# Other layouts for K and Q in DRAM, a single reciprocal load, wider gelus, new planner prices and a new order in a fused attention and mixer kernel

## The chip, the cores and the metric

The kernel runs on one core of a Trainium2 chip. The metric is device time in microseconds of one execution. The kernel before takes 1880.47 us, the median of three runs (1879.46 to 1881.93).

## The reference

The input x has 2048 tokens of 640 channels, in float32. It is normalised once (xn), and the output is x plus an attention block on xn plus a mixer block on xn.

```python
xn = layernorm(x)
# A: 32 heads of 20 channels
q, k, v = split(xn_n @ wqkv)              # xn_n = layernorm(xn)
o = softmax(q k^T * 20**-0.5) v           # per head, 2048 x 2048 scores
A = o @ wo
# B: spatial shift and MLP
h  = gelu(layernorm(xn) @ w1)             # 640 x 640
hs = shift(h, channels in 4 groups, tokens by +1, -1, +2, -2) @ w2
x1 = xn + hs
B  = x1 + gelu(layernorm(x1) @ w3) @ w4   # 640 x 1536 and 1536 x 640
out = x + A + B
```

## The kernel before

**Work and tiling.** TensorE multiplies fp32 numbers in a reduced format, so an operand is split into a high and a low part ("split": a rounding copy for the high part, a subtraction for the low part), and a product is three products (high-high, high-low, low-high). Two half-height products run side by side in the array ("twins"). Attention runs over 32 blocks: a block is a pair of heads and half of the tokens as queries (`HALF` = 1024), and has 32 units of work. A unit has two score products per head pair (`s`, followed by an exponential on ScalarE, ACT), two products that only look for the row maximum of a block that comes 14 to 43 units later (`pm`, followed by a maximum on VectorE, DVE), and one group of eight products with V (`pv`). Between these stand the products of everything else, as fill: Q, K and V (`ps_q`, `ps_k`, `psv`), w1, w2, w3, w4 (`ps`), and at the end wo (`pso`, `psl`).

**What goes through DRAM.** The Q and K projections are split, and both parts go into the DRAM tensors `qd` and `kd`, one per 128 channels, with the layout channel, block of 512 tokens, part, token. Per block, `load_q` fetches the two heads' Q for one half of the tokens into one of three tiles `zq`, three blocks ahead. Per pair of heads, `load_k` fetches all tokens of K into one of two tiles `kpack`. Both place three copies per head at different partitions: for Q the slots are high, low, high, for K high, high, low. A head has 20 rows; where they cross a boundary of 128 channels, each copy takes two transfers. The weights are split once and kept in DRAM: `prep` loads a piece (`ph_w`), rounds it on ACT or DVE, subtracts on GpSimd (POOL) and stores it as `wd_w`.

**End of a block.** `block_end` stores the block's four rows of sums (`od`), loads them again spread over 128 partitions (`sm`), takes reciprocals on DVE (`rc`), stores them (`rcd`), loads each of the four rows repeated over 32 partitions (`rb`, four transfers), multiplies on POOL and stores the result in `onm`.

**w1.** `w1_tile` computes 128 output channels for 2048 tokens, in two rounds of 1024. Each round evacuates two tiles into `pre` (two buffers of 1024 columns), multiplies by a row factor, runs one gelu on ACT, splits and stores to `hsd`. The gelu needs another table on ACT than the exponential, so each change loads a table. The last w1 tile and the last Q tile are computed in two visits, one round each.

**What sets the order.** All transfers are issued by one queue, SyncE (SP), in order. Nothing is ordered by hand except one string: a planner collects all operations, with a price each and the operations on which they depend, and simulates the engines in time. When an engine is free it takes the ready operation with the lowest key. For TensorE the string `ORDER` says at each step which kind comes next (`s` scores, `p` products with V, `m` maxima alone, `d` anything else). The planned order is then emitted on each engine. A transfer has a price for its issue on SP, a time on a shared bus (`xfer`) and a lateness (`late`: 3000 ns for the weight pieces and the end of a block, 1500 ns for Q and K), after which its users count as ready. The price of an issue is 375 ns, plus 100 ns from 128 runs and 130 ns more from 256 (line 620).

Line 356 holds every TensorE group, line 324 nearly every other operation, line 344 the small memsets with which the second half of a pair of twins waits for the first.

Of the kernel before, what the change touches and what calls it, by code (L numbers as in the profile page):

```python
# [21 lines left out]
P = 128  # L22
# [89 lines left out]
    "ddsdssdddssddsddssppppsdsddsdssddsddddsdddsddsddsdsddsdsdddsspdpppsddsdsdsddsdsddsddsdsdddsspssspppsdsddsdsdsd"
    "sddsddsdsddddsssdddsddsdddsddsdsddssddppppsdsdddsdssdddsddsddsdsddssdsddspsddsddsddsddsddsddspdsddsddsppppdsds"
    "ddsdsddsdsddsdspssdddsdsddsdsddsddsdsdddssdpspppsdsdddsdddddsdspssdddsdsdssdddsddsdsdsddsspssppsspssdddssddsdp"
    "dpssddddsdddsdsdddsdsdddssdddsddddsdsdddsddddssppsdddsdsdsdsdddsddsdsddssddppppssdddsdsdsddsdsddsdsddsdddddsds"
    "dsdsdsdsppppdsddsdssdddssdddsdddsdsdsdsddsdsdsddspssspsdsdddsdsppdddsddsddsdsddssdsdsdsddsddsdsppppssddsdsdsdd"
    "dsspdpsdsdddsdspdsdsddsdsddsdsdddsspssdddsddsdsdsdsdddsdsddsddddsdsppppsddssdddddsdsdsddssdddsdsdddssdddsddsds"
    "dsdpsddddsspppdsddsdsddssdsdsdddsspsspppsdsddssddsddssdddsdsddsddsddsdddssddsdsdddssppppdsdsdddsdsdddsdsddssdd"
    "sdsddssdddssppppsdsdddssddsdsdddsddsdddsssdddsdsddddsdsdddsdsddsssppppssdddsdsdsddsddsdsdsdsdddssppppsddsdsdsd"
    "ddssddsddsdsdsddddsddsdsdsdsdsddspdpppssddsdddssdsdddsdsdsddsddsdsdsddsdsppppsdsdddssdsddddssddsddddsssdddsddd"  # L120
    "ssddsddddsdsdsdpssspppddsdddsddsddsdsdsdsdddssdsddsdsddsdsppsddsdsddsdsddspsspssspssspssspsssdpssspssspssspsss"
    "psdsdddssdddddddsddddsssddddddsdddsdddssddddddddsdsdddddsdsdddppsddsddddsdddddsddddddddddsdsdddddddsdsppsddddd"
    "dddddsdsddddsddddddssppppdsddsddddddsssddddddsddddsdddddddsddddddsddppddddddsdddsddddsddsdsdddsdddddssddddddds"
    "ppddssdddsddsdddddsddsdssddddddsdddsdsdddddssddddddddddppppssdddsddsdddsddsddsdddsdsddsdddsddsdddddsddsppsspss"
    "spsdddsddsdddsdsddddddssddddssddddssdddddssdddddsddddsdppsdsdsppsssdddddsdddsppddsssdsssppssddddsdddsdddddsddd"
    "sssddddddddssddsdddddsddsdddsddssddsdsddsdddspppppsdsdddsdsddddsdsdddsddddddsddsdddddsddddssddddsddddsdsdddsdd"
    "dspppddddsdssdddddsdddddssdddsdsddsdsdsdsddsddsddsppppssdddssddsdsdddssddsdsddsdspdpppdsdssdddsddsddsdsdsddsdd"
    "sdddsddsdsdsdsddsdspppsdsdddssdddsdsdddsdddsdsddddssppppsdddsdsdddddddsddddsspssdddsdsdsddsddssddsdsdddssppsss"
    "ppsddsdsddsdsddsdsdsddsdddssddsdsdddssppppdsdsddssdddsdsddddsdsdsddsdsdddsdsdsdddssppppssddsddsddsddssdsddsddd"
    "sdddsdsdddsddsddsdddsddpppdsdddsdspssddsdddsdsddsdsdddsddsddsdddssddsdsddsdsppssppssdddsddsddssddsdsddsdddsspp"  # L130
    "ppdsdddsdssdddsddssddsddddsssddddsdddsddsdsddsdddspssppsspssssspssspssspssspssddddddssdsdddddsdddssdddddsdsdsd"
    "dddsddsddsppppsdsdddsdddssdddsddddsdsddsdsddsdddddsdddddsddsdddddssppdppdssddddsdddssdddsdddsddsdsddsdsddddddd"
    "dsddddddddddssdddddsddsddddsddddddddddddsddppppsdddsddddsddddssddddssdddsddddsdsdddsdddsdsppppsdsdddsdsddddsdd"
    "sdsdddsdddsdsddsdddsdsdddsdddddddddsdpppddsdddddddssddddsddsddpsdsddddssdddddsddsdsdddddsdsdddddsddsdddspdsdsp"
    "sdddssdddsddsdddsdddddddddsddsdppssspssddpssspsssssppsdsdddddddsspddssssspssspsssdddddsdsddsdssdddsdsddsppsddd"
    "sddsddsddddssddddddsdddsddsdddsdddddssppppdddddsddsddddssddddddsdddddddsdddddddssdddsddsddsddddsdddddddsdddsdd"
    "dsddddddsppdddddsdsdsdsddsddsdddssppppsdsddssddsddsdsdsddddddsssdddddssddsdsddsddsddsdppsssppsdsddssddsddsdsdd"
    "sdsdsddsdspppsdsddsdsddsddsdsddsddsddsppppdsddsddsddddddsdsdddsdspssdddsdsdsddsdsddsdsdsdddssppppssddsdsdddsds"
    "ddssdddsdddsssdddsdddsdsddssddsdddssdppppsdsddssddsdsddsdsddsdsddsdsppsdsddsdsddsdsdddsdsdddddsdddsddddsdspppp"
    "ddsdsdddsdsppsdsdsdsddsddsddssdddssddsdddddsdddssdsddsddsdddssppppssdddssdddsdsdsddsddsdddssddddsdsdsdddsspppp"  # L140
    "sdsdsdddsdssddsddsddsdsdddssdsdddsdspsssppssspssspsdpssspsdddsddspsddsdsddsddsdddsdddsddddddsddsdddsddsdsdsddd"
    "sppppddsdddsddsddddddsdsddsddsddddddddsddddsdddddddddddsdddssdsdddddsddddddsddsddddsdddsdddddsdsdppppssddddsds"
    "dddddssddddssdddsddsddddsdddsddddsdsddsdddppppdsdsdddddsddddsddsdsddddsdsddddsdddsddddsdssdddsdddppppsddddssdd"
    "dddsddsdsddddsdddsdddsddsdddssdddsdsdddsddsppppsddsdsddsddddsdddsdddsddsdddsdsddsddddsddsddsddsddsdppppsdsdddd"
    "dssdddsdddsdsddddsdsdddddsdsddsddsdddsdddddssppppsddsddsddddsddsdddssddddsdddddsddsdsdddddssdddddssddppppsdsdd"
    "sdddsddsdsddddddssdddddssddddssdddddsdddsddssddppppdsdsdsddddddssddsddsdddsdddddsddsdsddddssddddsddddssppppsdd"
    "dsdsdddssdddddsdddsdsdsdddddsdddssdddddsdsdddsddsppppsdddssdddddsdsddddsdddsddsdddsddsdsddddssdddsdddsddsdpppp"
# [1458 lines left out]
```

## Time and profile before

| | |
|---|---|
| median of three runs | 1880.47 us |
| the profiled execution | 1878.9 us |
| its span, first to last instruction | 1876.7 us |
| mean granted clock of TensorE | 0.994 |
| TensorE products (PE) busy | 1841.3 us, 98% |
| weight loads (PEld) busy | 1286.3 us, 69% |
| VectorE (DVE) busy | 1517.7 us, 81% |
| ScalarE (ACT) busy | 1389.4 us, 74% |
| GpSimd (POOL) busy | 446.9 us, 24% |
| moved by DMA | 257.80 MB, on average 137 GB/s |

A row of the profile names line, engine, operation, the tile written and the tile read, and the count. "Idle before" is the time an engine stood still before an operation, with the operation or transfer that ended the wait. The chain of waits follows the last instruction back to what released each step. A window gives the busy time of the engines in a stretch of the span, with the granted clock and the mean share of the 16 DMA engines that were busy. SPq is the queue of SyncE that issues the transfers; the times of its rows are those of the issue, not of the transfer.

### The profile page before, as it was taken

The page shows a single profiled execution, that of the slowest core. Times are in us where ns is not written, and L with a number is a line of the kernel's source. Part 1 is how long each engine was busy: PE and PEld are TensorE (multiplying, and loading weights), DVE is VectorE, ACT ScalarE, POOL GpSimd, SP SyncE. Part 2 cuts the span into 40 slices and gives each one's busy share as a digit, 9 for nine tenths or more (in the row PEclk, how much of TensorE's full clock was granted, in tenths as well). Part 3 has the DMA queues.
Part 4 walks back from the last instruction along what each step waited for, and adds up shares of the span by engine and source line. Part 5 has one row for each costly group of instructions (what it writes and reads, how often), then busy time and mean ns, then how long its engine had stood idle before and what let it go on. Part 6 is the DMA issues. An engine that isn't in the chain of part 4 may idle for free.

```text
span 1876.7 us, 44340 instructions
## 1 busy us (share of the span) xinstructions
PE 1841.3 (98%) x17153; PEld 1286.3 (69%) x17153; DVE 1517.7 (81%) x2696; ACT 1389.4 (74%) x2545; POOL 446.9 (24%) x665
## 2 busy tenths in 40 slices
PE   9999999999999999899999999999999999999998
PEld 7976776666666757567666757675777777776677
DVE  8888888897888989877779996778778778778624
ACT  5278777887888886668888776888677777778762
POOL 5112114423323223211112211112221222212211
PEclk9999999999999999999999999999999999999999
DMA  5764656536464586545325563344514242243402
GB/s 195 192 187 143 159 143 185 141 113 178 123 169 138 152 256 206 169 150 179 104 73 165 147 180 106 100 119 147 132 57 104 89 110 85 70 141 119 144 13 113
DMA packets 234243, 257.80 MB, mean 137 GB/s; under 512 B 60521, under 2 KB 175673, under 8 KB 234033
## 3 DMA queue, kind: packets, MB, share of 16 engines
q1 hardware_dynamic: 234032, 254.98, 46.2%
q8 instruction: 135, 2.21, 0.5%
q14 instruction: 76, 0.61, 0.1%
HBM read 151.64 MB, written 103.25 MB: 136 GB/s over the span
## 4 chain that ended last, share of the span: by engine, by line
PE 85%; DMA 6%; DVE 5%; ACT 1%; SPq 1%; POOL 1%; issue 1%; DVEq 0%; ACTq 0%; POOLq 0%
PE ps L356 24%; PE pv L356 22%; PE s L356 13%; PE pm L356 12%; PE psv L356 3%; PE pso L356 3%; PE ps_k L356 3%; PE ps_q L356 3%; DVE mx L324 3%; DMA ph_w<-in_B_w_dram 2%; SPq L324 1%; PE psl L356 1%; DMA kpack<-kd 1%; DMA sm<-od 1%; ACT p L324 1%
## 5 line engine op out<-in xcount | busy, mean ns | idle before, releaser
L324 DVE TENSOR_REDUCE mx<-pm 128x1 f32<-128x512 f32 x2048 | 1271.4, 682 | 215.5 <-PE pm L356 128.6
L324 ACT ACTIVATE p<-s 128x512 f32<-128x512 f32 x2048 | 1106.5, 604 | 199.7 <-PE s L356 78.5
L356 PE MATMUL s<-zq,kpack 62*128 62x512 f32 x2048 | 756.4, 409 | 14.0 <-ACT p L324 4.9
L356 PE MATMUL pm<-kpack,zq 60*128 60x512 f32 x2048 | 756.6, 409 | 8.4 <-ACT p L324 4.5
L356 PE MATMUL pv<-p,v 128*32 128x512 f32 x4096 | 487.3, 599 | 0.3
L356 PEld LDWEIGHTS s<-zq,kpack 62*128 62x128 f32 x2048 | 363.2, 186 | 119.4 <-DVE mx L324 30.7
L356 PEld LDWEIGHTS pm<-kpack,zq 60*128 60x128 f32 x2048 | 364.3, 186 | 104.2 <-DVE mx L324 30.0
L356 PE MATMUL ps<-xT,w_w 64*128 64x512 f32 x2040 | 329.6, 395 | 1.2 <-ACT p L324 1.2
L356 PEld LDWEIGHTS pv<-p,v 128*32 128x32 f32 x4096 | 120.8, 110 | 231.3 <-issue 198.6
L356 PEld LDWEIGHTS ps<-xT,w_w 64*128 64x128 f32 x2040 | 210.8, 188 | 37.4 <-issue 7.1
L324 POOL TENSOR_TENSOR ob<-ob,obq 128x512 f32<-128x512 f32 x96 | 125.2, 1304 | 322.3 <-ACT obq L324 284.7
L356 PE MATMUL ps<-xT 64*128 64x320 f32 x1632 | 170.6, 308 | 0.1
L356 PEld LDWEIGHTS ps<-xT 64*128 64x128 f32 x1632 | 146.8, 186 | 13.2 <-issue 2.5
L324 ACT COPY obq<-pv 128x512 f32<-128x512 f32 x83 | 48.8, 588 | 125.2 <-PE pv L356 124.9
L344 POOL MEMSET scratch<- 1x1 f32 x134 | 12.9, 96 | 458.7 <-PE ps L356 294.2
L356 PE MATMUL ps<-xT,gT 64*128 64x320 f32 x1152 | 121.9, 307 | 0.0
L356 PEld LDWEIGHTS ps<-xT,gT 64*128 64x128 f32 x1152 | 104.1, 186 | 8.0 <-issue 1.7
L356 PE MATMUL psv<-wv,xT 64*128 64x320 f32 x960 | 93.4, 309 | 0.8 <-ACT xT L324 0.8
L356 PEld LDWEIGHTS psv<-wv,xT 64*128 64x128 f32 x960 | 82.0, 186 | 8.4 <-issue 3.0
L356 PE MATMUL ps_q<-xT,w_q 64*128 64x512 f32 x480 | 83.2, 400 | 0.0
L356 PE MATMUL ps_k<-xT,w_k 64*128 64x512 f32 x480 | 80.3, 397 | 0.9 <-POOL scratch L344 0.9
L356 PE MATMUL pso<-wos,oT 64*128 64x320 f32 x768 | 67.5, 308 | 0.0
(182 smaller groups left out, 1393.2 us busy)
## 6 DMA issues: line engine op xcount, KB each, us to landing
zq<-qd SPq DMA_DIRECT2D x156, 80.0 KB
kpack<-kd SPq DMA_DIRECT2D x78, 160.0 KB
w_w<-wd_w SPq DMA_DIRECT2D x48, 256.0 KB
gd<-pre SPq DMA_DIRECT2D x8, 1536.0 KB
g<-gd SPq DMA_DIRECT2D x64, 192.0 KB
wd_w<-ph_w SPq DMA_DIRECT2D x34, 320.0 KB
xT<-wd_w SPq DMA_DIRECT2D x34, 320.0 KB
vd<-vst SPq DMA_DIRECT2D x32, 256.0 KB
```

Source lines behind the costliest of these rows:

```text
L324: o.insts = [getattr(e, m)(val(out), *[val(x) for x in ins], **{k: val(v) for k, v in kw.items()})]
L344: o.insts = [nc.gpsimd.memset(scratch.get(), 0.0)]
L356: o.insts = [nc.tensor.matmul(out.get(), lhsT.get(), rhs.get(), **kw) for out, lhsT, rhs, kw in products]
```

## The change

Five things change.

1. `qd` and `kd` get the layout channel, half of the tokens, part, 1024 tokens. A load of K then reads two runs of 4 KB per row instead of four of 2 KB, a load of Q one run instead of two. A store of 512 tokens writes two runs of 2 KB per row instead of one of 4 KB. Where a head's 20 rows lie in one tensor, its first two copies of Q (high and low) come in one transfer, whose DRAM side runs over part, row, token.
2. The four loads of `rb` become one, whose DRAM side runs over 4 rows, 32 repeats, 512 columns.
3. In `w1_tile` one buffer `pre` of 2048 columns stands for a whole column tile, and the gelu runs once per visit: over 2048 columns for the first four tiles, over 1024 twice for the last one.
4. The planner has other prices: own issue times for several transfers, other limits for the rest, and other prices for a few DVE operations (`bn_stats`, `bn_aggr`, one `tensor_scalar`).
5. `ORDER` is another string of the same length, 7039 letters, with the same number of each letter.

```diff
 ORDER = (
-    "ddddddddddddddddddddddddddddddddddddddddddddddddddddddddddddddddddddddddddddddddddddddddddddddmddddddddddddddd"
...
+    "ddddddddddddddddddddddddddddddddddddddddddddddddddddddddddddddddddddddddddddddddddddddddddddddddddddddddmdmddd"
...
-    def dma(o, i, nbytes, es=2560, **kw):
+    def dma(o, i, nbytes, es=2560, iss=None, **kw):
         n = nbytes / es
-        op_ = pl("dma", 375.0 + 100.0 * (n >= 128) + 130.0 * (n >= 256), "dma_start", o, i,
+        op_ = pl("dma", iss or (375.0 if n < 128 else 425.0 if n < 256 else 630.0), "dma_start", o, i,
                  xfer=1.1 * (8.0 + 0.0375 * es) * math.ceil(n / 16), **kw)
...
-    qd = [dt([P, 4, 2, 512], F32R, f"qd{c}") for c in range(ND)]
-    kd = [dt([P, 4, 2, 512], F32R, f"kd{c}") for c in range(ND)]
+    qd = [dt([P, 2, 2, HALF], F32R, f"qd{c}") for c in range(ND)]
+    kd = [dt([P, 2, 2, HALF], F32R, f"kd{c}") for c in range(ND)]
...
-            pl("dve", 402.0, "bn_stats", st[:, j, :], src[:, j * 320:(j + 1) * 320])
-        pl("dve", 81.0, "bn_aggr", mv, st)
+            pl("dve", 357.0, "bn_stats", st[:, j, :], src[:, j * 320:(j + 1) * 320])
+        pl("dve", 110.0, "bn_aggr", mv, st)
...
-        o = dma(raw[:, :n].rearrange("p (k c) -> p k c", k=k), src, n * 512, 4 * n // k)
+        o = dma(raw[:, :n].rearrange("p (k c) -> p k c", k=k), src, n * 512, 4 * n // k, 480.0)
...
-                kept[nm, tb] = dma(_f(dst[:, tb]), _f(hl), 524288, 4096)
+                kept[nm, tb] = dma(_f(dst[:, tb // 2, :, tb % 2 * 512:tb % 2 * 512 + 512]), _f(hl), 524288, 2048, 560.0)
...
+        pres = {}
+
         def w1_tile(nm, w, ts=(0, 2)):
             c = int(nm[3:])
+            if c not in pres:
+                pres[c] = wp.tile([P, S], F32, tag="pre", name=f"pre1_{c}", bufs=1)
+            pre = pres[c]
             for t2 in ts:
-                pre = wp.tile([P, 512 * W1B], F32, tag="pre", name=f"pre1_{c}_{t2}", bufs=W1N)
...
-                pl("act", c_act(512 * W1B, False), "activation", pre, pre, AF.Gelu_apprx_tanh, table="gelu")
-                for b in range(W1B):
-                    tt = t2 + b
+                if t2 != ts[-1]:
+                    continue
+                a = pre[:, ts[0] * 512:(t2 + W1B) * 512]
+                pl("act", c_act((t2 + W1B - ts[0]) * 512, False), "activation", a, a, AF.Gelu_apprx_tanh, table="gelu")
+                for tt in range(ts[0], t2 + W1B):
...
 def load_k(pair):
-                        rdma(_f(t[b:b + n, s]).rearrange("p (c t) -> p c t", c=4), _f(src[r0:r0 + n, :, part, :]), n * S * 4)
+                        rdma(_f(t[b:b + n, s]).rearrange("p (c t) -> p c t", c=2), _f(src[r0:r0 + n, :, part, :]), n * S * 4, 4096)
 def load_q(blk):
-                for slot, part in enumerate(SLOT_Q):
+                slots = list(enumerate(SLOT_Q))
+                if n == DH:
+                    b = 64 * e
+                    rdma(_f(t[b:b + 2 * DH, :]), _f(src[r0:r0 + n, qh]).rearrange("p q t -> q p t"), n * HALF * 8, 4096)
+                    slots = slots[2:]
+                for slot, part in slots:
                     b = 64 * e + slot * DH + o
-                    rdma(_f(t[b:b + n, :]).rearrange("p (c t) -> p c t", c=2),
-                         _f(src[r0:r0 + n, qh * 2:qh * 2 + 2, part, :]), n * HALF * 4)
+                    rdma(_f(t[b:b + n, :]), _f(src[r0:r0 + n, qh, part, :]), n * HALF * 4, 4096)
...
-        for r in range(4):
-            adma(rb[32 * r:32 * (r + 1), :], rcd[blk, r:r + 1].to_broadcast([32, 512]), 65536, LATE)
+        adma(rb, rcd[blk].unsqueeze(1).to_broadcast([4, 32, 512]), 262144, LATE)
         pl("pool", c_pool(512), "tensor_mul", rb, ob, rb, port=True)
```

More of the change, by code (lines that the diff above doesn't have):

```diff
@@ new lines @@
+    "dmddddmddmdddddmddddmddddddmdddddddddddmddddddddddmddddddddmmmddddddddddddddddddmddmddddddddddmmdddddddddddmdd"
+    "dddddddddmddddddddmmmddddddddddddddddddddmddddddddmddmmddddddddddddddddmdddddddddddddmddmdddddddmdddddddddddmd"
+    "ddmdddddddddmsddddsddddddddsdddddsdddsddsdddsdddsddssdddsddddssdddddsddmdddsddsdsdddmsppppsdsddssdddsdssdddsds"
+    "dsddsdsdsddsdsdddsmppppsddsddssddsddsdsddsddsddssddsdsddsddmsdpssppdssddddsdsddspsdsdddsdsdsddsddssddsdddssppp"
+    "psddsddssddsddsdsdddssdddsspsspppsdsddssddsddsdsddsdsddddsssddddsdsddsdsdsddsdsppssdddspsssppssspsdsdddddsdspd"
@@ new lines @@
+    "psddsddddddsssddddsddddddsddsdddddsddddsdddsdssdddddssdddddssddddsddddsdsdppppdsdsdsdddsddddsdddddsssdddddddsd"
+    "dssdddsdddsppppsdddssdsddddsddddsdddssddddssddddsdddsdddssdpssspppsdddsdssddddddssdddddssddsdddsdddddssddddddd"
+    "dsddssddppppddssdddddddsssdddddddsddsddddddsddsddsddddsdsdsddddsdsppppdssdddsddsddddsddddsdddddsddddsddsdsdddd"
+    "ssddddsdsddsdddsddddssppppsddddssddddsdssddddssdddssddsddssdddsddssddsddddsppppssdddsddssdddssdddssdddsdsppdss"
+    "dddsddsddsdsddsddsddsdsdpppssspsdsddsdsppsdsdsdsdsddsdsdddsdssddssdddssdddssddsdsspdddsdspppssdddsdsddsdsddsds"
@@ new lines @@
+    "dsdsdddssppppssdsdddssdddssdddssddsddddsdsdddsddsdsddsdsdppppsddssddsdssddsdddsdsdsdddddsdsdsdppsssppdsddsdddd"
+    "ddddsddsdddsssddddsddssddsddsdsdsddsdsppppssddsdsddsdsddsdddsdsdsddssddsdsddsdddssppppssdddssddsdsddddsdsddsdd"
+    "ssdddsdsdsdsddpppssddddsddsdsddsdsddsdsdddddsspssdsdsdsdsddppppsddsddssddssdssdddddssddsdsdspssdppsspdssddsdsd"
+    "psdddddsdsddddsddsdddssdddsddsddsdddsdsdddsdspppssddsddsddsddssddsdsdddsdsdppppsdsddsddsdsdsdddssdsdddddsddsds"
+    "dsddsdsppppsdsddssdddsdssddddssddsdddssdsddsdsddspssspssddddsddsdddsdppdsdddssdsdsdsdsdsdsdddssppppssddsdsdsdd"
@@ new lines @@
+    "dsspdpssddddsdspdsdsdddsdpsddssdddssdsddsdsddsdddssddsdsdddssppppssdddssddsddsddsdsdsddddsssddddddsdssdddsdsdd"
+    "sdsdppppssddsddsddsddsdssddsdddsdssddsppppsdsdsddsdsddsdsdddsddsdsdssdsdsdsddsdddssdpdpppsddssddssddsdsddsdsdd"
+    "spssddpsdsppsdsdsddsdddsddddsdddddsdddsssdddddsdsddssdddssddsdsdppsssppsdsdsdsdddsdsddsdsdsdsddsdsppppsdsddsds"
+    "dsdddsdsddsddsdsdddsdddsdsdsddsdspdpppssddddsdssddsdsddsdsddsdsdddsdsdsdsppppdsdssdddsdsddsdsdsdddddsssdddddsd"
+    "ssdddsddsddsdsdpssspppddsdsddddddssddsdsdddssdddsdssddsddssppssdddsdsdddsspsspssspssspssspssspdssspssspssspsss"
@@ new lines @@
+    "pssddddsddsddddsdddddsssddddsdddddddsddsddddsddddsdddddsddsddppppsdsdddssdddsddsddddddddsddsddddsdddddddssdddd"
+    "dsddddddddddsdsdddddsppppsdddsddddddsssdddddddsdsdddddddsddddddddsddppdddsddddsddddsddddsddsdddsdsdddsddddddds"
+    "ppsddsdddddsddsddddsddssdddsdsdddsdsdddsddddddddddssddddpppsspssdddsdddsddsddddsdddssdddddsdddsdddsddddppsssps"
+    "sspsddddsddsdddsddddsddssdddsdddsdddsdddsddddsdddddsddsppsssddppssdsdddddddsspddspssssspdpsdsdsddsdsdddddsddsd"
+    "ddsssddddsdddddsdsdsddddddddsdsddsdddsdssddddpppppsdddsdsddddsdddddddsdddddsdsdddsddsddddssdddsddddsdsdddsddsd"
@@ new lines @@
+    "dspppsddddddsdsddddsddddssdddsdsddssdddsdsddsddssdppppssddsddsddssdddsdsdsdsdddssppppdsddsdssdddsdddssddsdddsd"
+    "ddsdsddsddsdsdsddsdsdddsspppssdddsddsddsddsddsddsddsppppsddddsddddsdddsdsdddspsdsddssddsddsddssddsdsddsdsppsss"
+    "ppdsdsddssdddssdddssdddsddssdsddsddsdsppppdsdsdsdsddsdsdddsdddsdsddsdsdsddsdsdsddsdsppppdssddsddsdsddsdsdsddds"
+    "ddsddsddsddsdsdsdddsdddssdppppdsdddsddsdsdsdddsdsddddsdsdsddsdsddsdsppppsdsddssdddssdsddsddsddsddssdddsddssddp"
+    "pppddsssddddsdsdsddsdddddsssddddsddssdddsdsdsddddssssppssppsssspssspssspssspsddsdsdddddsdsdddsdddssddsdddddsdd"
@@ new lines @@
+    "ssddddddssppppsdsddsdsdddddsddsddddssdsddddsddsddddsdddsdsppdsddddsddsdddsdddsdddsppsddsddsdsddddssddddddsddds"
+    "ddddddsddddddssdddddddsdsdddddddddddddddsddppppdsdsddsdddddsdsdddddssddddsddsddsdddsddddssppppsdsdsdsdddsddddd"
+    "sdsdddssddsddsdddddsdddsdddddddddssddpppddsdddddddsddsdddddsdpsdsdsdddsdddsdddsddsddsdddsddsddddsddddsdspssddp"
+    "sddsdsddsdddsddsdddddsdddddddsdsppspssspssddpssspdsdddsddddsspsspddsssssspssspssddddsdsddssdddsdsdsddsdsppsdsd"
+    "ddsddddsdsdddsdddddsdddsdsdddddssddddsppppddsdsddddddsdsdddsddddddddssdddddsdsddddssdddsdddsddddssdddddsdddddd"
@@ new lines @@
+    "dssddddddddsppppsddsdddddddsdsppsdddsdddsdsdddsddssddsddsddddsssddddsdsddddsdsddssdddspppssspssdddssddsdsdddss"
+    "ddsdsddsdspppsdsddsdsddsddsdsddsddsddspdpppsddsddsddddddsdsddddsspssdddssdddssddsdsddsdsddsdsppppssdddsdsdsdsd"
+    "dsdddsdsdddsssdddsddsddsddsdsddsdsdsdppppsdsddsdsdsddsdsddsdsdsddsdsppsdsdddsdsdddsdsddsdsdddsdddsddddssdppppd"
+    "ddsdsdddsdsppdsdsdsdsdddsdsdsdsdddsdsdddsddsddsdddsdsdsdsddsdsppppsdsddsdsddssddsdddssdddsdddsdsddsdsddsdspppp"
+    "sdsddsdsddssddddssdddssddsdsddsddsdspssspssspppssssdpssspsdsddddddsspsdsddsddddsdsdsddsddddddsdsdddsddddsdddsd"
@@ new lines @@
+    "sppppdssdddsdddsdddddsdddssddddddsdddsddddddsdddddsddddsdddddsdsddddddddddsdssdddsdddddddddppppddddsssddddddds"
+    "ddsddddsdddsddsddsddddsdddsdsddsddsddddssppppdssddsdddddssdddddsdsdddddsdsdddsdddsddddsddssddsddppppdssddsddsd"
+    "ddddsddddsddsdsddddddsddsdsddddsdsddddssddppppssddddssdddsddsddddddssddddddsdsdddssdddddssdddddssdppppsdsddddd"
+    "dssdddddsddsdsddddsddssdddddsdddssdddsddsddsppppsddsddssdddsddddddsddsddsddsddddsdsdsdddddsddsddddssppppddssds"
+    "ddddddsdsdsdddsdddsddddsdsddddsdsddddsddsdsdddsppppdsddsddsddsdddsdsdddsdsddddddsdddssddddsdsdddsdddsdsppppdsd"
@@ new lines @@
+    "dsdddssdddsddddsdsdddsdsddddsdddssdddddsddsddsddsppppsdsdddsddddssdddsdddddsdssdddddsddsdsdddddssddddddssppppd"
+    "ssddddssddddsdsdddddsdsddddssdddsddddsdddsdsddsddddssppppsddsddsdsddddssdddsdddsdddsdddsdsddsdddsdddsddsddddss"
+    "ppppsdsdddsdddsdsdddsdddsdddsdsddsddddssdddddsdsddsddddssppppsdddsddsdsdsddddsddddsdddssddsddddsdddddssdppppsd"
+    "sddddddsssddddddsddsddddsdsdsddddsddddsddsddsddsddsddsdddsdsppppdsdsdsddsdddsdddsddddsdsdddsdddsddddsdddssddsd"
+    "ddddssppppssdddsddsddddsddsddsdddsdddsdsdddsdsddddsddsddddddssppppsdsddsdddsdsdddsddsddsdddddsdsdddsdddsdsdppp"
@@ new lines @@
+    "pdsdddsddsdddssdsddddsdddsddsdsddddddsddsddsddddsdsdddsdsddddsdsdppppsdsdddsddsdsddddsddddsddsddsdsdddsddddsds"
+    "ddddsddsdsdppppsdsddsdddddsdddsddsddsdddssddddsdddsddddssdsddddsddsppppssdddsddsddsddsdddsdddsddddsddsdsddddds"
+    "spppdpsddsdsddddddsssdddddddssdddddssddddsddddsdddsdsddsddddssddddsdsdppppsddsdddddsdsdddssddddsddddsdsdddsdds"
+    "ddddsdsdsddddsdsppppsddsddsdddsdsdddsdsdddddsdsdsdddddsddddssddsdddsddsdppppssdddsdddsddddssdddddsdddsdsdddsds"
+    "ddddddssdppppsdddsddddsssddddddddsddsdddssddddsddddsdsddsddddssddsddddddssppppssddddsdddsddssddddsddsdsdddddss"
@@ L779, in prep @@
         w = dt([P, 2, n], F32R, "wd_" + name)
-        dma(_f(w), _f(hl[:, :, :n]), n * 1024, 8 * n if n == 320 else 4 * n).late = PREP
+        dma(_f(w), _f(hl[:, :, :n]), n * 1024, 8 * n if n == 320 else 4 * n, 480.0).late = PREP
         wdone[name] = w
@@ L1053, in w1_tile @@
                     tb = t2 + b
-                    v = pre[:, b * 512:(b + 1) * 512]
+                    v = pre[:, tb * 512:(tb + 1) * 512]
                     evac(v, ps, 512)
@@ L1057, in w1_tile @@
                        alt=("dve", c_dve(512), "tensor_mul", True))
-                pl("act", c_act(512 * W1B, False), "activation", pre, pre, AF.Gelu_apprx_tanh, table="gelu")
-                for b in range(W1B):
-                    tt = t2 + b
+                if t2 != ts[-1]:
[3 more added lines that the diff above has]
+                for tt in range(ts[0], t2 + W1B):
                     t0, t1 = tt * 512, (tt + 1) * 512
                     hl = st1.tile([P, 2, 512], F32R, tag="hl", name=f"hlh_{c}_{tt}", bufs=HLB)
-                    split(hl[:, 0], hl[:, 1], pre[:, b * 512:(b + 1) * 512], 512)
+                    split(hl[:, 0], hl[:, 1], pre[:, t0:t1], 512)
                     for g in range(4):
@@ L1070, in w1_tile @@
                         r = slice(lo - c * P, hi - c * P)
-                        dma(_f(hsd[c][r, :, a:e]), _f(hl[r, :, a - sh - t0:e - sh - t0]), (hi - lo) * 4096, 2048)
+                        dma(_f(hsd[c][r, :, a:e]), _f(hl[r, :, a - sh - t0:e - sh - t0]), (hi - lo) * 4096, 2048, 640.0)
         jobs = ["k2", "w1_0", "q2", "w1_1", "k3", "w1_2", "q3", "w1_3", "k4", "w1_4", "q4"]
@@ L1112, in hs_load @@
                         r = slice(lo - k * P, hi - k * P)
-                        dma(_f(hs[k][r, :, a - t0:e - t0]), _f(hsd[k][r, :, a:e]), (hi - lo) * 2048, 1024)
+                        dma(_f(hs[k][r, :, a - t0:e - t0]), _f(hsd[k][r, :, a:e]), (hi - lo) * 2048, 1024, 640.0)
             return hs
@@ L1366, in tile_kernel, with adma @@
     fill["on"] = False
-    def adma(o, i, nbytes, late=0.0, es=2048):
+    def adma(o, i, nbytes, late=0.0, es=2048, iss=None):
         k = pl.key
         pl.key = k + K_DMA
-        r = dma(o, i, nbytes, es)
+        r = dma(o, i, nbytes, es, iss)
         r.late = late
@@ L1375, in adma, with rdma @@
         return r
-    def rdma(o, i, nbytes):
-        adma(o, i, nbytes, 1500.0)
+    def rdma(o, i, nbytes, es=2048):
+        adma(o, i, nbytes, 1500.0, es)
     def rows(src, head):
@@ L1482, in max_fin @@
         for e in range(2):
[L1483 removed]
+            adma(_f(zq[blk % 3][64 * e + 60:64 * e + 62, :]), mv[e], 8192, es=4096, iss=300.0)
     last, obs = {}, {}
@@ L1493, in block_end @@
         n = 2 * HALF // P
-        adma(od[blk], ob[DH:P:32, :], 8192, LATE)
+        adma(od[blk], ob[DH:P:32, :], 8192, LATE, 2048, 600.0)
         pl.key += REST
```

78 lines of the change are left out of this document (11 added, 67 removed).

## The prediction

> **What bounds the kernel now.** I read the page first: span and busy shares.
>
> ```profile
> span 1876.7 us, 44340 instructions
> PE 1841.3 (98%) x17153; PEld 1286.3 (69%) x17153; DVE 1517.7 (81%) x2696; ACT 1389.4 (74%) x2545; POOL 446.9 (24%) x665
> ```
>
> TensorE (PE) has work 98% of the span, and no product is added or removed. What can move is the 35.4 us in which PE is idle (1876.7 - 1841.3) and the stretches at a lower granted clock. The windows, cut around each gap, show where they lie (columns: width, then busy us of PE, PEld, DVE, ACT, POOL, then clock, DMA share of 16 engines, GB/s).
>
> ```profile
> 328.00:338.00 10.00, 6.92 (x34) 4.78 (x32) 6.61 (x13) 8.05 (x13) 3.44 (x4) 0.66 0.49 135
> 440.00:450.00 10.00, 6.06 (x34) 2.69 (x36) 3.94 (x8) 3.79 (x8) 2.41 (x3) 0.66 0.31 85
> 664.00:672.00 8.00, 5.00 (x30) 4.29 (x28) 4.40 (x8) 3.72 (x8) 0.39 (x2) 0.79 1.11 308
> 771.00:781.00 10.00, 5.33 (x28) 2.50 (x26) 3.54 (x7) 4.11 (x8) 0.86 (x1) 0.66 0.66 230
> 405.00:407.00 2.00, 1.02 (x7) 0.53 (x7) 2.00 (x4) 1.15 (x3) 1.35 (x2) 1.00 0.22 48
> 581.00:583.00 2.00, 1.06 (x10) 0.59 (x8) 1.83 (x4) 1.94 (x4) 2.00 (x3) 1.00 0.06 13
> 1335.00:1338.00 3.00, 1.36 (x12) 0.66 (x8) 1.82 (x4) 1.98 (x3) 0.43 (x1) 1.00 0.19 57
> ```
>
> The first four hold 3.08 + 3.94 + 3.00 + 4.67 = 14.7 us of idle PE, and clock lost on top: 0.34 x 10 three times and 0.21 x 8, 11.9 us. Together at most 26.6 us, since part of the slow clock falls in the idle time. The last three rows (0.98, 0.94, 1.64 us idle) lose no clock. The chain of waits, then the timelines of ACT and DVE, say what the long gaps waited for.
>
> ```profile
> 322.33 6.45 DMA ph_w<-in_B_w_dram
> 437.50 6.16 DMA ph_w<-in_B_w_dram
> 660.38 6.44 DMA sm<-od
> 769.09 6.21 DMA ph_w<-in_B_w_dram
> ```
> ```profile
> 328.86 0.40 ACT L324 CAST ph_w<-ph_w 128x256 fp32r<-128x256 f32 x1 [4.50 <-DMA ph_w<-in_B_w_dram]
> 443.55 0.61 ACT L324 CAST ph_w<-ph_w 128x128 fp32r<-128x128 f32 x2 [4.75 <-DMA ph_w<-in_B_w_dram]
> 666.85 0.25 DVE L324 RECIPROCAL rc<-sm 128x16 f32<-128x16 f32 x1 [3.75 <-DMA sm<-od]
> 775.37 0.46 ACT L324 CAST ph_w<-ph_w 128x320 fp32r<-128x320 f32 x1 [7.21 <-DMA ph_w<-in_B_w_dram]
> ```
>
> One picture four times: an in-order engine stands at a cast or reciprocal whose load has not landed, the exponentials or maxima queue behind it, their PSUM tiles stay full, PE stops. Each late load was issued behind the burst with which SP fetches the next Q and K.
>
> ```profile
> L324 SPq DMA_DIRECT2D zq<-qd x204: 247/329/1099, 43.3 to 1686.3; - x102
> L324 SPq DMA_DIRECT2D kpack<-kd x102: 584/742/1351, 70.9 to 1639.3; - x102
> L324 SPq DMA_DIRECT2D kpack<-kd x15: 587/742/882, 535.7 to 650.6; - x15
> L324 SPq DMA_DIRECT2D ph_w<-in_B_w_dram x70: 332/424/1856, 240.6 to 806.1; - x70
> 1632.75 2.18 SPq L324 DMA_DIRECT2D zq<-qd  x6
> 1634.98 5.10 SPq L324 DMA_DIRECT2D kpack<-kd  x6
> 1637.00:1640.00 3.00, 3.00 (x34) 1.68 (x28) 1.10 (x3) 1.41 (x4) 3.00 (x2) 1.00 0.63 137
> 658.00:664.00 6.00, 6.00 (x53) 3.36 (x47) 4.16 (x8) 5.94 (x8) 2.35 (x2) 1.00 1.05 372
> ```
>
> The third row is the window from 480 to 700 us (bursts at 536 and 645); the ph_w loads end at 806. A burst costs SP 2.18 + 5.10 = 7.3 us. The next-to-last row has only such loads in flight: 20 rows each, and 0.63 x 16 = 10 engines work, at 137/10.1 = 13.6 GB/s per engine; the last row gives the best rate here, 372/16.8 = 22.1.
>
> **Part by part.** *K by halves.* Each kpack load has 40 runs of 4 KB instead of 80 of 2 KB. The old zq load is 20 rows of two runs, the same form, at 0.329 us of SP. So a kpack issue costs between 0.329 and 0.742; I take 0.33, the same shape. Six save 6 x 0.41 = 2.5 us per burst. Bytes stay.
>
> *Q.* 52 pairs of loads become one (whole heads; heads split over two tensors stay), so 204 issues become 152: two fewer per burst, 0.7 us. With K, loads behind a burst are issued about 3.1 us sooner. The merged one walks DRAM as 2 x 20 x 1024, priced on SP between 0.329 and 0.742. What it does to the engines is the rival below; here I take +2 us (0 to +23.5).
>
> *The planner's prices.* It plans both kinds at 375 ns; kpack measured 742. So a plan is 6 x 0.37 = 2.2 us early after each burst and puts a cast on ACT that much before its data can be there. Faster K issues and truer prices both work on the same 3.75 to 7.21 us waits: 2.2 to 3.1 us off each. Off four gaps of 14.7 us that leaves 14.7 - 4 x 2.6 = 4.3 us idle, and gaps under 1.7 us kept the clock at 1.00, so nearly all 11.9 us of clock would return too: up to -22. But a moved order makes new meetings of casts and late loads; I take half, -11 (0 to -26.6).
>
> *One reciprocal load instead of four.*
>
> ```profile
> L324 SPq DMA_DIRECT2D rb<-rcd x120: 302/419/1617, 176.4 to 1762.0; - x120
> L324 POOL TENSOR_TENSOR rb<-ob,rb 128x512 f32<-128x512 f32 x30 | 39.1, 1303 | 28.5 <-DMA rb<-rcd 27.4 <-issue 0.7
> 721.09 4.66 DMA rb<-rcd
> ```
>
> SP saves 3 x 0.419 = 1.3 us per block, 38 us in all, hidden because SP does not set the end outside bursts. If four outer rows mean four engines, 262,144 B take 65.5 KB/22.1 = 3.0 to 4.8 us instead of about 1. POOL waits for it (27.4 us now) and is idle 76% of the span; queued behind on POOL are the low halves of weights and the additions into ob. Once (721 us) that reached the chain. I take +1 (0 to +9: three such meetings, 3 us each).
>
> *Stores of Q and K in two runs.*
>
> ```profile
> L324 SPq DMA_DIRECT2D qd<-hl_q x16: 319/344/1560, 164.4 to 688.1; - x16
> L324 SPq DMA_DIRECT2D hsd<-hlh x32: 519/605/1087, 333.6 to 672.1; - x32
> ```
>
> Forty stores go from 0.344 towards the two-run form's 0.605: +0.26 each, 10 us of SP over 660 us. Nothing reads them soon, so 0 on the path; without that cover, +1.
>
> *w1's gelu by column tiles.*
>
> ```profile
> L324 ACT ACT_TABLE_LOAD x37 | 47.5, 1283 | 1.5 <-PEq L1593 0.7
> L324 ACT ACTIVATE pre<-pre 128x1024 f32<-128x1024 f32 (+1 forms) x18 | 32.7, 1818 | 0.2
> 400.43 1.28 ACT L324 ACT_TABLE_LOAD   x1
> 401.72 1.06 ACT L324 ACTIVATE pre<-pre 128x1024 f32<-128x1024 f32 x1
> 402.80 1.28 ACT L324 ACT_TABLE_LOAD   x1
> ```
>
> Now each of ten gelus holds ACT 3.63 us. Four column tiles go from two to one; the last keeps two, as it is computed in two visits. So 10 become 6, and 8 table loads go. The wide form (3072 columns) takes (32.7 - 10 x 1.06)/8 = 2.76 us, 0.83 ns a column, so 2048 columns take 1.91 and the hold is 4.47: 4 x (7.26 - 4.47) = 11 us of ACT. On the path lies only what PE lost in a hold: about 1 us each at 405 and 581 (the hold quoted ended just before 405). I take -1.5 (from -3 to +3.4, if each longer hold stops PE 0.84 us more). The single buffer makes the next tile's evacuation wait for the splits of this one; a Q or K tile lies between.
>
> *The order.* Both strings have 7039 letters of the same counts. The runs of p fall from 213 to 209, and each run costs a change of PE's mode.
>
> ```profile
> 410.19 0.99 PE pv L356 x8
> 640.84 3.57 PE pv L356 x32
> 644.41 0.43 PE s L356
> 636.63 0.23 PE s L356
> ```
>
> Four groups at once take 3.57, one alone 0.99, so a group is 0.86 and a run adds 0.13; the first s after it takes 0.43, where others take 0.23. Four runs fewer: -1.3 (0 to -1.3).
>
> *Sum:* -11 - 1.5 - 1.3 + 1 + 2 = -10.8. The profiled execution took 1878.9 us (span 1876.7 and 2.2 around it): 1868.1. The median, 1880.47, lies 1.6 above it, so I predict **1870**.
>
> **The rivals.** *A: the bursts still make loads late, but about half is recovered: 1870,* own range 1860 to 1876. For it: all four long gaps follow a burst, and SP's share in it is mispriced and shrinks. Against: the burst at 536 us already passed without a long gap, so chance decides part.
>
> *B: no change, 1878.* A burst moves 6 x 80 + 6 x 160 = 1440 KB at 137 GB/s, 11 us whatever SP does. If the landing of the load behind is set by these bytes, an earlier issue only waits longer, and -1.3 - 1.5 remain.
>
> *C: slower, the merged Q load runs on few engines: 1901.* Loads of 20 rows ran on 10 engines. A two-row load looks like this:
>
> ```profile
> 1367.00:1368.00 1.00, 1.00 (x11) 0.56 (x8) 0.07 (x1) 0.36 (x1) 0.00 (x0) 1.00 0.07 16
> ```
>
> That is zq<-md, two rows of 4 KB twice, on 0.07 x 16 = 1.1 engines. If the outermost count sets the spread, the merged load, outermost count 2, puts 81,920 B on each of two engines. Two of them and the two third-part loads are 180,224 B there, 8.2 us (at 22.1) to 13.3 us (at 13.6), against 49,152 B, 2.2 to 3.6 us, now: 7.8 us more, ahead of every later load that uses all engines. Against the 3.1 us sooner issue that leaves +4.7 for each of the five bursts between 300 and 770 us, while the weight loads ph_w run: +23.5, less 2.8. It decides as soon as the added lateness exceeds 3.1 us and the cast has no more slack than the waits above show. Against it: Q-only bursts have no load that waits so closely, and after 806 us the loads have longer to land. The Trainium skill says just this in "DMA: Bandwidth & Descriptors", sections on the increment of 16 and "Rules for kernel authors": the engine count is the largest up to 16 dividing both sides' outermost sizes, and a small outermost size "confines the whole DMA" to that many. The 0.63 row agrees for 20 rows; for the merged shape no run here shows it yet.
>
> *D: every late load after a burst disappears: 1851* (1880.5 - 26.6 - 1.3 - 1.5). For it, the long gaps share one cause; against, only 2 to 3 us of each 4 to 7 us wait is priced above.
>
> **How the numbers follow.** A 0.43, B 0.15, C 0.30, D 0.12. A measurement of this kernel can tell some 0.2%, 3.8 us, from no change. Faster: A and D, 0.55; same: B, 0.15; slower: C, 0.30. Range 1853 to 1899: it leaves out half of D and about half of C, and so contains the bounds of all single terms but C's. Of the signs, A and D alone would give 1850 to 1876.
>
> **What would show it.** SP's kpack issues near 0.33 us and a burst under 4 us (K and planner right). ACT and DVE waits for ph_w and sm behind bursts below 3 us, windows there at clock 1.00 (A). DMA share near 0.12 while only merged Q loads fly, and waits of 8 us behind them (C). Table loads 29. If the four long gaps come back elsewhere with the same 6 us loads, A is wrong and B right; if the time moves without these gaps moving, the whole reading is wrong.

## The result and the profile after

The changed kernel takes 1928.67 us, the median of four runs (1928.08 to 1929.33), beside 1881.2 us for the kernel before (four runs beside it). The ratio is 1.0254, with a 95% interval from 1.0236 to 1.0271: it is slower by 47.5 us. The forecast was 1870 us, with a range up to 1899 us.

The page of the profile after, its first lines:

```profile
span 1926.4 us, 44100 instructions
PE 1861.3 (97%) x17153; PEld 1295.4 (67%) x17153; DVE 1512.6 (79%) x2691; ACT 1382.0 (72%) x2540; POOL 446.2 (23%) x663
```

The same 17153 products take a span that is 49.7 us longer. Idle time of PE is 1926.4 - 1861.3 = 65.1 us, 29.7 more than before. The other 20.0 us are busy time: the products are the same, and the mean granted clock fell from 0.994 to 0.981. The windows of the changed kernel around its longest gaps (columns as before: width, busy us of PE, PEld, DVE, ACT, POOL, clock, DMA share, GB/s):

```profile
210.00:220.00 10.00, 5.93 (x36) 4.96 (x37) 3.49 (x7) 4.63 (x10) 0.75 (x2) 0.66 0.60 151
445.00:456.00 11.00, 5.92 (x26) 2.77 (x27) 4.67 (x8) 4.66 (x9) 1.96 (x2) 0.69 0.82 211
562.00:572.00 10.00, 4.25 (x23) 3.09 (x23) 4.23 (x9) 3.40 (x7) 0.00 (x0) 0.66 0.41 128
800.00:811.00 11.00, 5.77 (x42) 4.82 (x42) 4.11 (x7) 4.51 (x9) 1.75 (x3) 0.69 0.63 209
1147.00:1159.00 12.00, 6.61 (x38) 5.34 (x36) 4.57 (x8) 4.01 (x8) 0.00 (x0) 0.72 0.72 213
1275.00:1285.00 10.00, 5.91 (x31) 4.46 (x30) 5.30 (x9) 3.09 (x6) 0.00 (x0) 0.66 0.29 86
```

The kernel before had four such windows, all before 781 us. Here they go on to 1285 us, and these six hold 4.1 to 5.8 us of idle PE each. What ended the waits, from the timelines of PE, ACT and DVE:

```profile
804.82 0.46 ACT L324 CAST ph_w<-ph_w 128x320 fp32r<-128x320 f32 x1 [5.79 <-DMA ph_w<-in_B_w_dram]
1153.13 2.07 PE L356 MATMUL ps<-xT,w_w 64*128 64x512 f32 x8 [5.39 <-DMA w_w<-wd_w]
1278.53 0.25 DVE L324 RECIPROCAL rc<-sm 128x16 f32<-128x16 f32 x1 [8.00 <-DMA sm<-od]
```

Beside the weight pieces ph_w it is now also weights that PE waits for itself (w_w) and the reciprocals' input. The chain of waits shows where the time before that went, and SP's timeline what stood there. The first line is from the chain of the kernel before, the others are from the changed kernel:

```profile
762.38 6.69 DMA kpack<-kd
```
```profile
782.33 13.37 DMA kpack<-kd
795.77 6.15 DMA wd_w<-ph_w
1258.01 12.33 DMA kpack<-kd
1270.40 6.55 DMA od<-ob
```
```profile
779.70 2.59 SPq L324 DMA_DIRECT2D zq<-qd  x4
782.33 8.96 SPq L324 DMA_DIRECT2D kpack<-kd  x6
794.81 0.35 SPq L324 DMA_DIRECT2D v<-vd  x1
```

A K load that took 6.7 us in the kernel before takes 12 to 13 us in these two bursts. The first of them occupies SP for 11.6 us (779.70 to 791.29), and SP then issues nothing for 3.5 us. The list of SP's waits names what it stands for. In the kernel before this line reads 0.3 us, once:

```profile
SPq L324 <- DMA zq<-qd: 81.9, 29, 4.3
```

29 times SP itself waited for a Q load to land before it could issue the next transfer, 81.9 us in all. This wait is the program's own. In the traces the transfers take eight semaphores strictly in turn, and SP waits for a semaphore's last transfer before it issues the next one on it; the planner reckons with this (`LANES = 8`). The fifth K load of the burst (issued at 789.77) and the load of V (794.81) stand eight places behind the two merged Q loads. They are the two places at which SP stood, 7.6 us together.

Where hardly anything else is in flight, the transfer engines show what the merged loads do. This window lies behind a burst without K, whose four issues began at 1734.80 us and were over by 1737.5:

```profile
1741.00:1745.00 4.00, 4.00 (x50) 3.82 (x48) 4.00 (x8) 3.87 (x8) 1.30 (x1) 1.00 0.13 50
```

0.13 of sixteen engines is 2.1, so two engines, at about 25 GB/s each. They were still at it ten microseconds after the first issue. The single reciprocal load, with an outermost size of 4, ran on four (0.26 x 16 = 4.2), again at 25 GB/s each, while it flew alone:

```profile
1754.00:1755.00 1.00, 1.00 (x14) 1.00 (x14) 1.00 (x2) 1.00 (x3) 0.04 (x1) 1.00 0.26 100
```

The issue times and the other edits, from the lists by tile and by line:

```profile
L324 SPq DMA_DIRECT2D zq<-qd x152: 242/464/950, 44.8 to 1736.8; - x152
L324 SPq DMA_DIRECT2D kpack<-kd x102: 583/739/1199, 71.0 to 1690.8; - x102
L324 SPq DMA_DIRECT2D rb<-rcd x30: 567/588/881, 173.6 to 1809.2; - x30
L324 ACT ACT_TABLE_LOAD x29 | 37.2, 1283 | 1.5 <-PEq L1602 0.7 <-DVE pre L324 0.2
L324 ACT ACTIVATE pre<-pre 128x2048 f32<-128x2048 f32 x4 | 7.7, 1914 | 0.0
POOL rb L324 <- DMA rb<-rcd: 41.3, 13, 9.9
```

A K issue takes 0.739 us with 40 runs of 4 KB, as it took 0.742 with 80 of 2 KB. Table loads fell from 37 to 29, and a gelu over 2048 columns took 1.914 us in the mean of four. GpSimd waits 41.3 us for rb, where it was 27.4.

### The profile page after: what moved, and what is told of

Its sections match the earlier page's. It is cut to its first block, busy times and chain, and to the rows that moved or that the text cites. A ratio compares the mean times of both kernels' runs of the same rounds, so it can differ in the third digit from the quotient of the medians.

```text
span 1926.4 us, 44100 instructions
## 1 busy us (share of the span) xinstructions
PE 1861.3 (97%) x17153; PEld 1295.4 (67%) x17153; DVE 1512.6 (79%) x2691; ACT 1382.0 (72%) x2540; POOL 446.2 (23%) x663
## 4 chain that ended last, share of the span: by engine, by line
PE 81%; DMA 10%; DVE 4%; ACT 2%; SPq 1%; issue 1%; POOL 1%; DVEq 0%; ACTq 0%; POOLq 0%
PE ps L356 23%; PE pv L356 20%; PE s L356 12%; PE pm L356 12%; PE psv L356 3%; PE pso L356 3%; DVE mx L324 3%; PE ps_q L356 3%; PE ps_k L356 3%; DMA kpack<-kd 2%; DMA ph_w<-in_B_w_dram 2%; SPq L324 1%; PE psl L356 1%; DMA zq<-qd 1%; DMA od<-ob 1%
## 5 line engine op out<-in xcount | busy, mean ns | idle before, releaser
L356 PE MATMUL ps<-xT,w_w 64*128 64x512 f32 x2040 | 344.0, 401 | 5.4 <-DMA w_w<-wd_w 5.4
L356 PEld LDWEIGHTS ps<-xT,w_w 64*128 64x128 f32 x2040 | 222.8, 191 | 41.8 <-issue 10.4
```

The costliest lines, as they stand in the source:

```text
L356: o.insts = [nc.tensor.matmul(out.get(), lhsT.get(), rhs.get(), **kw) for out, lhsT, rhs, kw in products]
```

## The experiments

Theory 1 is rival C of the prediction: the merged Q load, whose outermost size is 2, sits on two engines and holds up all behind it. Theory 2 blames the new order and prices. Theory 3 blames the one reciprocal load, whose outermost size is 4. The first three runs keep the changed kernel's plan on every engine: only the transfers that SP issues in a planned place differ. Ratios are to the kernel before, timed beside each group of runs; the edits are shown abridged.

**Two Q loads in the place of the merged one.**

```diff
-  rdma(t[b:b + 2*DH, :], src[r0:r0 + n, qh].rearrange("p q t -> q p t"), ...)
+  # planned as before; issued as
+  dma_start(t[b:b + DH, :], src[r0:r0 + n, qh, 0, :])
+  dma_start(t[b + DH:b + 2*DH, :], src[r0:r0 + n, qh, 1, :])
```

> The changed kernel with the same plan on every engine; only where it issues one merged Q load (2 x 20 rows of 4 KB), SyncE issues two loads of 20 rows each. Theory 1 (the merged load sits on two of the sixteen transfer engines and holds up all that is queued behind it): most of the 47.5 us goes, 1880 to 1893 us, no stretch at a DMA share of 0.12 behind a burst. Theory 2 (the new order and the new prices are to blame): 1915 us or more. Theory 3 (the reciprocal load on four engines is to blame): 1920 us or more.

Measured: 1872.15 us beside 1879.96, ratio 0.9957 (0.9939 to 0.9975). With 52 more issues on SP and not a byte less, the kernel passes from 2.5% slower to 0.4% faster than before. Its page and the new loads' issue times:

```profile
span 1863.7 us, 44174 instructions
PE 1838.4 (99%) x17153; PEld 1279.2 (69%) x17153; DVE 1512.4 (81%) x2691; ACT 1380.7 (74%) x2540; POOL 446.0 (24%) x663
L1411 SPq DMA_DIRECT2D zq<-qd x104: 272/322/1143, 43.3 to 1672.5; - x104
```

PE idles 25.3 us instead of 65.1 (this profile is of the fastest of six executions), and SP's waits for Q loads fall to 1.7 us, in four waits. The time lies 8 us below the range expected by theory 1: more than the loss is gone. Theory 1 holds; theories 2 and 3 fail as the main cause.

**Four reciprocal loads in the place of one.**

```diff
-  adma(rb, rcd[blk].unsqueeze(1).to_broadcast([4, 32, 512]), 262144, LATE)
+  # planned as before; issued as
+  for r in range(4): dma_start(rb[32*r:32*(r+1), :], rcd[blk, r:r+1].to_broadcast([32, 512]))
```

> The changed kernel with the same plan; only where it issues the one reciprocal load, SyncE issues four loads of one row repeated over 32 partitions, as the kernel before. Theory 1: little, 1920 to 1929 us. Theory 2: the same. Theory 3: 1895 us or less, and the waits of GpSimd for rb fall from 41 us below 27 us.

Measured: 1921.99 us, ratio 1.0232 (1.0192 to 1.0272). That cannot be told from the changed kernel's 1.0254. GpSimd still waits 35.6 us for rb, far from the fall below 27 that theory 3 asked for.

**Both at once.**

> Both of the above at once, same plan. Theory 1: as with the two Q loads alone, within 6 us, 1876 to 1893 us. Theory 2: 1915 us or more; what is left over 1881 us belongs to the order, the prices, the gelu and the layout.

Measured: 1863.54 us, ratio 0.9914 (0.9883 to 0.9945), 12 us below the range expected, and in a second comparison, below, 1868.93 us, 0.9934 (0.9910 to 0.9957). With two Q loads, the single reciprocal load seems to cost some 0.2 to 0.4%, 4 to 8 us, but the intervals overlap with that of the two Q loads alone, so this is not shown. The page of the first:

```profile
span 1856.9 us, 44286 instructions
PE 1834.6 (99%) x17153; PEld 1278.1 (69%) x17153; DVE 1507.4 (81%) x2691; ACT 1379.2 (74%) x2540; POOL 445.5 (24%) x663
```

Idle PE is 22.3 us, 13 us less than in the kernel before. In the profile of the second comparison it is 26.7 us (1869.9 - 1843.2), 9 us less. Either way the rest of the change is a gain.

**One merged Q load, with the rows outermost.** The same 160 KB in one transfer, but DRAM is walked row, part, token. High and low parts then lie on alternate partitions, so the two high copies of K go to every second partition, and the placing of the first block is changed to match. The planner plans this kernel anew, so a few operations move between engines (VectorE 2685 instructions instead of 2691).

```diff
-  rdma(t[b:b + 2*DH, :], src[r0:r0 + n, qh].rearrange("p q t -> q p t"), ...)
+  rdma(t[b:b + 2*DH, :], src[r0:r0 + n, qh], ...)                     # 20 rows outermost
-  K and part-heads: partitions b .. b + n
+  K and part-heads, slots 0 and 1: partitions 64*e + 2*o + slot, step 2
```

> The changed kernel with the merged Q load kept as one transfer of the same 160 KB and as many issues, but with the 20 rows outermost and the two parts inside, so that the copies lie alternately on the partitions; the copies of K go to every second partition to match. Theory 1 (the outermost count sets the number of engines): 10 engines instead of 2, DMA share near 0.6 while it flies, 1880 to 1895 us. If merging as such or the order is to blame: 1915 us or more.

Measured: 1872.45 us, ratio 0.9961 (0.9943 to 0.9980), below the range expected, as with two loads. A burst of the same kind as above (two merged and two third-part loads, issued from 1578.83 to 1581.67 us, the next transfer at 1583.07) shows how many engines work:

```profile
1581.00:1582.00 1.00, 1.00 (x12) 0.29 (x12) 1.00 (x2) 1.00 (x1) 0.00 (x0) 1.00 0.56 197
1582.00:1583.00 1.00, 1.00 (x16) 0.33 (x12) 1.00 (x3) 1.00 (x3) 0.54 (x1) 1.00 0.51 131
```

0.56 and 0.51 are 9 and 8 engines, near the ten expected and far from two. SP's waits for Q loads are 0.8 us, once. So merging as such is harmless; the outermost size of 2 was not.

**The merged load alone, in the kernel before.** Plan, order, prices, gelu and reciprocal loads are the old ones; K and Q lie by token halves, and where the first copy of a whole head was loaded, both come at once, parts outermost.

> The kernel before with its own plan, order, prices, gelu and four reciprocal loads; only K and Q lie by token halves and the first two copies of a whole head's Q come in one transfer, parts outermost. If the merged load alone is the cause whatever the order is: some 40 to 55 us slower than before, 1920 to 1935 us. If it hurts only together with the new order: within 15 us of before.

Measured: 1925.21 us, ratio 1.0232 (1.0216 to 1.0248). One window behind a burst without K, SP's wait, and the issue time:

```profile
1740.00:1745.00 5.00, 5.00 (x57) 4.87 (x59) 4.55 (x8) 4.50 (x9) 1.29 (x1) 1.00 0.13 51
SPq L324 <- DMA zq<-qd: 79.7, 28, 4.7
L1405 SPq DMA_DIRECT2D zq<-qd x52: 629/672/867, 43.3 to 1736.1; - x52
```

The same two engines, the same waits of SP, and a loss of like size (44.6 us here, some 56 us in the changed kernel), with the old order and plan as with the new ones. The layout by token halves, which this run has too, is worth nothing by itself, as a run below shows. The issue of a merged load costs 0.672 us, as much as the two that it replaces (0.32 each), so it did not even save time on SP.

**What the rest of the change is worth.** Each run takes one part back in the version with two Q and four reciprocal loads.

```diff
-ORDER = (the new string)
+ORDER = (the string of before)
```

> The version with two Q loads and four reciprocal loads (some 16 us under the kernel before), with the order string of the kernel before. If the new order holds that gain: 1876 to 1884 us. If the gain is the gelu's, the prices' or the layout's: 1860 to 1868 us.

Measured: 1893.49 us, ratio 1.0077 (1.0054 to 1.0100), slower than the kernel before by 0.8%, beyond the range expected. I read this as the old string not fitting the new plan; how much the new order is worth by itself this run can't say.

```diff
-  iss or (375.0 if n < 128 else 425.0 if n < 256 else 630.0)
+  375.0 + 100.0 * (n >= 128) + 130.0 * (n >= 256)
-  bn_stats 357, bn_aggr 110, tensor_scalar 520
+  bn_stats 402, bn_aggr 81, tensor_scalar 430
```

> The same version with the planner's prices of the kernel before, the new order kept. If the truer prices hold the gain: 1874 to 1884 us, with waits of 4 us and more for ph_w behind a burst. If not: 1860 to 1868 us. An order that was found with other prices may also fit them badly, which gives the same reading, so this run can acquit the prices but not convict them alone.

Measured: 1880.79 us, ratio 1.0004 (0.9985 to 1.0023). The gain is gone. The sign named is there too: ACT waits 5.45 us for ph_w at 773 us, behind a burst, and 5.74 us at 675 us, where with the new prices ACT's longest wait for ph_w is 3.1 us (4.6 us in that version's second profile). As the expectation said, that may be the prices or the misfit between them and a string found with others, and these two runs cannot separate the two.

```diff
-  pre: one buffer of 2048 columns, one gelu per visit
+  pre: two buffers of 1024 columns, one gelu per round
```

> The same version with w1's gelu in two rounds of 1024 columns, as before (37 table loads). By the prediction's term: 1.5 us slower, between 3.4 us faster and 3 us slower. If the gelu holds the gain: 1874 us or more.

Measured: 1875.52 us, ratio 0.9971 (0.9954 to 0.9988). Against 0.9914 and 0.9934 for the version with wide gelus, the wide form with this string is worth about 0.4 to 0.6%, 7 to 11 us, more than the 3 us that I allowed. Again the string came with the wide form, so how much of this is the gelu's own is not shown, and the interval touches that of the second comparison.

```diff
-  qd, kd: [P, 2, 2, 1024], loads in runs of 4 KB, stores in two runs of 2 KB
+  qd, kd: [P, 4, 2, 512], loads in runs of 2 KB, stores in one run of 4 KB; plan unchanged
```

> The same version and the same plan with K and Q in DRAM by blocks of 512 tokens: loads in runs of 2 KB, stores in one run of 4 KB. By the prediction a K issue costs 0.41 us more here; but the K issue measured 0.739 with 40 runs as with 80, so by the runs so far the layout is worth nothing on SyncE: 1860 to 1868 us, issue 0.74. If the longer runs make the transfers faster: 1870 us or more and a lower rate per engine in a burst.

Measured: 1866.35 us, ratio 0.9933 (0.9911 to 0.9954), the same as with the new layout; the K issue is 0.742 us. The layout by itself is worth nothing that can be measured.

**Can the version be planned better?** It was repeated beside two versions that plan what is issued.

> The version with two Q loads and four reciprocal loads once more, beside the next two: 1858 to 1868 us.

```diff
+  for r in range(4): adma(rb[32*r:32*(r+1), :], ..., 65536, LATE)      # planned as four
+  for slot, part in enumerate(SLOT_Q): rdma(...)                       # planned as three
```

> The same transfers as that version, but the planner knows them: it plans two Q loads and four reciprocal loads, so what it plans on the other engines moves a little while the order string stays. A truer plan should be no worse: 1855 to 1868 us. A string that fits its old plan closely should be worse: 1870 us or more.

```diff
-  rdma(K, n * S * 4, 4096)
+  rdma(K, n * S * 4, 4096, 740.0)
```

> The last one with the K issue priced at 740 ns, as it measured, instead of 375. If the price of the K issue is what makes loads behind a burst late: 2 to 10 us faster than the last one. If the string's fit counts more: slower than it.

Measured, in this order: 1868.93 us (0.9934, 0.9910 to 0.9957), 1 us above the range expected, 1876.29 us (0.9971, 0.9960 to 0.9982), 1870.64 us (0.9935, 0.9921 to 0.9949). The plan that knows its transfers is worse by 0.4%, and the intervals just lie apart: in this one case the string's fit counted for more than the truth of the plan. With the plan changed in both, the true price of the K issue brings 0.36%, 5.7 us, and these intervals lie apart too. Its trace shows what the price does: with 375 ns ACT waits 9.9 us in three waits for ph_w, up to 6.0 us, and with 740 ns no engine waits for a load of ph_w. (One of the five timings of that last kernel was 4593.8 us; what happened in it is not known. The other four have a median of 1869.4 us, and the ratio leaves it out.) The fastest version is the one with two Q and four reciprocal loads, with either layout, 0.7 to 0.9% under the kernel before and 3% under the changed one.

## Why the prediction was wrong

**The step that failed** is the term "Q" in the sum: +2 us, with what the merged load does to the engines put off to rival C. The merged load alone costs 2.32% in the kernel before, 44.6 us, and taking it out of the changed kernel moves the ratio by 0.0297, some 56 us; the term's upper bound was 23.5 us. The mechanism was described rightly in rival C, with its place and its cause, and held by every sign named there: share 0.12 to 0.13 while only such loads fly, and waits of up to 8 us behind them. The rule of the Trainium skill quoted there ("DMA: Bandwidth & Descriptors", the section on the increment of 16) agrees with these runs: with an outermost size of 2 the load ran on two engines and 25 GB/s each, and with 20 rows outermost the loss was gone.

**Its chance was mis-set.** Before any run, the row of 0.63 for 20 rows already bore the mechanism out. What I set against it was that few loads would wait behind it. That was an assumption on slack, taken only from the four gaps that the kernel before had, and those were left over by a plan that expected the old duration.

**Its price was mis-sized,** 1901 instead of 1929. The time of the loads was not the error: 180,224 B at the measured 25 GB/s are 7.2 us, and the forecast said 8.2 to 13.3. I counted 4.7 us of added lateness at five bursts up to 770 us. Three things were left out.

- Other bursts hurt as well. After 806 us w_w and sm came late (5.39 us at 1153 us, 8.00 us at 1278 us). Behind bursts without K, which I took to be harmless, ACT waited 4.24 us at 617 us and 3.60 us at 855 us.
- The lateness falls into the clock: all six windows shown have a clock of 0.66 to 0.72. The 49.7 us of the span are 29.7 us of idle time and 20.0 us of slower products, and C had nothing for the second part.
- SP waits itself for the slow loads, 81.9 us in 29 waits, as its eight semaphores go round. So the burst does not end 3.1 us sooner but several microseconds later (11.6 us of issue instead of 7.3, and 3.5 us of standing still).

**K by halves: wrong.** The K issue was to fall to 0.33 us and stayed at 0.739; the "same shape" as an old Q load did not decide. The 2.5 us per burst and the 3.1 us sooner never came.

**Q issues: wrong.** Two issues of 0.32 became one of 0.67.

**Late loads behind a burst, -11 us: neither of its two grounds came.** The K issue did not get faster, and the changed planner still prices it at 375 ns, since its 40 runs are fewer than 128 and no price of its own is given. So the plan stays 2.2 us early per burst. The version with two Q and four reciprocal loads does gain 12 to 16 us, and the sum without the terms of these loads has -13.8 (-11 - 1.5 - 1.3). But that agreement is luck: the wide gelu brings 7 to 11 with its string instead of 1.5, the layout nothing, and order and prices can only be seen together. One version bears out the mechanism that the term names: where the K issue was at last priced at 740 ns, the waits for ph_w were gone and the kernel was 5.7 us faster.

**One reciprocal load, +1 us (0 to +9):** 4 to 8 us by the difference of two runs, inside the range, but not clear of the noise. It ran on four engines, as the prediction supposed. Its issue costs 0.588, so a block saves 1.1 us of SP and not 1.3, and GpSimd's wait rose to 41.3 us. **Table loads** fell to 29 and the gelu took 1.91 us, as worked out; only its worth on the path came out larger than the term, with this string. **The stores** rose from 0.344 to 0.392 us (median), less than the 0.605 feared; 0 on the path was not tested alone, but the layout as a whole is worth nothing.

## What to carry to other kernels

Before two transfers are merged, look at the outermost size of the DRAM side: a window in which only such loads fly shows how many engines they use, as its DMA share times sixteen. Here sizes of 2, 4 and 20 gave two, four and eight to ten engines, and the size of 2 made a slow transfer in spite of its runs of 4 KB. A slow transfer costs its users little if they have slack, but what is issued behind it lands late, and where semaphores go round, as here, the issue itself stops; so price it by what is issued in the next ten microseconds, not by who reads it. And when a rival's mechanism is already borne out by a row of the trace, its chance should not be argued down by slack that no row shows.

## What was not expected of the hardware

The issue of a K load costs 0.74 us with 80 runs of 2 KB and with 40 of 4 KB. Two Q loads of 20 rows cost 0.32 us each, the merged one 0.67. The loads of the last part of wo cost 0.74 as well, with 40 runs of 1280 B. Neither bytes nor runs alone explain these, and what does is left open.

SP stood still for transfers that it had issued itself (81.9 us for Q loads, 0.3 us in the kernel before), although it only issues and does not use the data. That is no limit of the hardware but the program's eight semaphores; what more of them would be worth was not tried.
